# Sliding-window attention with a gated feed-forward: one P times V visit for two units, weights in half tiles

## The chip, the cores and the metric

One core of a Trainium2 chip. The metric is device microseconds of one execution, lower is better; times are medians of several runs. Engines are named as the profile names them: PE (TensorE) and PEld (its weight loads), DVE (VectorE), ACT (ScalarE), POOL (GpSimd), SP (SyncE, which issues nearly all DMAs here).

## The reference

All float32, T = 2048 tokens, D = 512, 32 heads of 16, window W = 256, F = 1792.

```python
xn = layernorm(x)                                   # no scale, no shift, eps 1e-5
q, k, v = split(xn @ wqkv)                          # 32 heads of 16
scores = q @ k.T / 4, kept where 0 <= i - j < 256   # else -1e9
s = concat_heads(softmax(scores) @ v) @ wo
f = (silu(xn @ w_gate) * (xn @ w_up)) @ w_down
return x + s * silu(f)
```

## The kernel before

**Precision.** A float32 matrix is split into two F32R tiles, high = copy to F32R (ACT) and low = value - high (POOL for weights and hidden tiles, DVE for what comes from PSUM). A product is three matmuls, the pairs (high, high), (high, low), (low, high) of `PAIRS`. P times V is done in plain float32, for which the trace shows two matmul records per call.

**Row halves.** PE is used as two halves of 64 rows, r = 0 and r = 1, that work side by side. Each dense item is summed in one bank, first by r = 0, then by r = 1 some `LAG` = 7 matmuls behind; a one-column DVE copy (`handover`, tile `ho`) separates the two. Weight tile j holds the upper input rows of unit j in partitions 0 to 63 and the lower ones of unit j - 1 in 64 to 127, so r = 0 reads tile n and r = 1 tile n + 1 during unit n.

**Dense work.** Tokens go in four chunks of 512. Per chunk there are 30 units in an order made by `dense_order`: `Proj` (q and k of a group of heads, tile a), `Values` (vp), `GateUp` (tiles g and u), `Down` (d, in four quarters of the hidden blocks and two halves of the output columns) and `Wo` (s). `Stationary` units (Proj, GateUp) hold weights in PE and move 512 tokens: item 0 uses the first 512 columns of the weight tile, item 1 the rest. `Moving` units (Values, Down, Wo) move 256 columns of weights, and both items use the whole tile. Each item takes one of four banks (`fb_free`).

**Weights.** `w_fetch` loads a raw tile (wr, 128 x 1024), `w_split` makes high (wh) and low (wl) of it in two or three cuts. Raw, high and low tiles all come from one pool of `NWB` = 10 tiles of 4 KB a partition; a pair is freed when both row halves are through with the unit (`unit_end`).

**Attention.** A unit u is four heads in one chunk, 32 units in all. For each: `max_pair` (scores b, row maxima on DVE, tile jk), `max_turn` (transposes the maxima, ms goes into q by a DMA of 8 KB), `prob_pair` (scores c with the maximum as an extra row, exponentials p on ACT, masks on POOL at L1325 and L1329), and `pv_visit` (P times V with v and a column of ones, L1390). All of these share four banks (`rb_free`). `pv_visit` uses PE as eight tiles of 64 x 32, issues all its matmuls in a row with nothing between them, and its two banks, one per row half, are added on the way out: copy on ACT (L1406), add on DVE (L1411), tile ev. ev goes to DRAM (od). The probabilities lie in one buffer of `PCAP` = 7168 columns: a unit's 6144, and 1024 more.

**Denominators.** `reciprocals` fetches the sums of two units from od, inverts them, stores them in rd. `o_prep` loads o from od and r from rd, and makes the operand of `Wo`.

**Order.** The program is a list in a fixed order on every engine, made ahead of time by a planner in the kernel itself. It keeps a virtual clock, costs per instruction, queues for DVE, ACT, POOL and DMAs ordered by due times (`do`, `dma`), and streams of attention visits with due times in units of dense work (`plan_attention`). An attention visit is put between dense matmuls when it is due and ready; dense work goes on where no visit is. Slots of 2 KB (`NSL` = 14, `take` and `give`) hold what lives for a short time.

Of the kernel before, what the change touches and what calls it, by code (L numbers as in the profile page):

```python
# [37 lines left out]
NHID = 8  # L38
PCAP = 7168
NSL = 14  # L40
NWB = 10
# [4 lines left out]
SPARE = 3  # L46
# [8 lines left out]
LEAD = 1.05  # L55
# [7 lines left out]
def tile_window_attention_swiglu_gate(  # L63
# [259 lines left out]
    def load_first():  # L323
# [66 lines left out]
        def split(raw, j, r, t):  # L390

            def high(a):
                if j not in wtile:
                    wtile[j] = [w_take(f"w{'hl'[s]}{j}", F32R) for s in range(2)]
                nc.scalar.activation(wtile[j][0][half(r), a : a + 512], raw[half(r), a : a + 512], AF.Copy)

            def low(a):
                hi, lo = (w[half(r), a : a + 512] for w in wtile[j])
                nc.gpsimd.tensor_tensor(lo, raw[half(r), a : a + 512], f32(hi), op=ALU.subtract)
                if r == 0 and a:  # L400
                    w_give(raw)

            def ready(t):
                if (j, r) == (1, 0):
                    low1.append(t)
                else:
                    wready[j] = t
# [12 lines left out]
        wr = [w_take(f"wr{j}", F32) for j in range(2)]  # L420
# [8 lines left out]
        split_next[0] = 2  # L429
# [48 lines left out]
    class Unit:  # L478
# [3 lines left out]
        def wts(self, r):  # L482
            return wtile[self.n + r]
# [10 lines left out]

    wfree = [f"w{i}" for i in range(NWB)]
    wheld = {}

    def w_take(name, dtype):
        tag = wfree.pop(0)
        t = pers.tile([P, 1024], dtype, name=name, tag=tag, bufs=1)  # L500
        wheld[id(t)] = (t, tag)
        return t

    def w_give(t):
        wfree.append(wheld.pop(id(t))[1])

    split_next = [0]

    def w_fetch(j):
# [8 lines left out]
        def go(r, u, last):  # L518
            if not box:
                box.append(w_take(f"wr{j}", F32))  # L520
# [7 lines left out]
        for n, (r, u) in enumerate(parts):  # L528
# [3 lines left out]
                slack=1.0, can=lambda: box or len(wfree) >= 3)  # L532

    def w_split(j, t, raw):
# [3 lines left out]
        if max(w) > both:  # L538
            r = 0 if w[0] > both else 1
            cuts += [(half(r), a, min(a + 512, max(w))) for a in range(both, max(w), 512)]  # L540
        if j not in weighted:
            cuts = [(half(1), 0, 256), (slice(0, P), 256, 768), (slice(0, P), 768, 1024)]
        left = [len(cuts), len(cuts)]

        def high(pr, a, b):
            if j not in wtile:
                wtile[j] = [w_take(f"w{'hl'[s]}{j}", F32R) for s in range(2)]
                split_next[0] += 1
            nc.scalar.activation(wtile[j][0][pr, a:b], raw[pr, a:b], AF.Copy)  # L549

        def low(pr, a, b):
            hi, lo = wtile[j]
            nc.gpsimd.tensor_tensor(lo[pr, a:b], raw[pr, a:b], f32(hi[pr, a:b]), op=ALU.subtract)  # L553
            left[1] -= 1
            if left[1] == 0:
                w_give(raw)

        def done(t):
            left[0] -= 1
            if left[0] == 0:  # L560
                wready[j] = t
# [7 lines left out]
        for n, (pr, a, b) in enumerate(cuts):  # L569
            do("S", t, 0.13 + 0.00078 * (b - a), lambda pr=pr, a=a, b=b: high(pr, a, b),  # L570
               lambda t, pr=pr, a=a, b=b, n=n: do(
                   "G", t, 0.17 + 0.0021 * (b - a), lambda: low(pr, a, b), done, before(MG, n)), before(MS, n),
               lambda: j in wtile or (split_next[0] == j and len(wfree) >= 2))


# [3 lines left out]
    def w_end(j):  # L579
        for t in wtile[j]:  # L580
            w_give(t)

    def unit_end(j, t):
        if (0, j) in half_ended and (j == 0 or (1, j - 1) in half_ended):
            timer(t, w_end, j)
# [53 lines left out]
    class Stationary(Unit):  # L639
# [7 lines left out]

        def gate(self, i, r, m):
            return xready.get((self.c, m // 3)) if self.n == 2 and i == 0 else 0.0

        def mms(self, i, r, pb):
            w = [t.rearrange("p (a k n) -> p a k n", a=2, k=KC) for t in self.wts(r)]
            xs = xn[self.c % 2]
            for k in range(KC):
                for a, b in PAIRS:
                    def go(first, last, k=k, a=a, b=b):
                        mm(pb, w[a][half(r), i, k, :], xs[b][half(r), k, :], first, last)
                    yield 512, go

    class Proj(Stationary):  # L660
# [7 lines left out]
        def done(self, i, pb, t, free):  # L668
# [3 lines left out]
            def high():  # L672
                tiles.extend(take(f"qk{'hl'[s]}{c}_{g}", dtype=F32R) for s in range(2))
                nc.scalar.activation(tiles[0], pb, AF.Copy)

            def low():
                nc.vector.tensor_tensor(tiles[1], pb, f32(tiles[0]), op=ALU.subtract)
# [7 lines left out]
            def after_high(t):  # L685
                do("V", t, 0.61, low, after_low, PRIO)
# [10 lines left out]
            do("S", t, 0.52, high, after_high, PRIO, can=room(2))  # L697

    class GateUp(Stationary):
# [8 lines left out]
        def done(self, i, pb, t, free):  # L708
# [7 lines left out]
            if i == 0:  # L716
                def tanh():
                    self.th = take(f"th{c}_{fb}")
                    self.y = take(f"y{c}_{fb}")
                    nc.scalar.activation(self.th, pb, AF.Tanh, scale=0.5)  # L720

                def one():
                    nc.vector.scalar_tensor_tensor(
                        self.y, self.th, 1.0, pb, op0=ALU.add, op1=ALU.mult
                    )
                    give(self.th)
# [5 lines left out]
                do("S", t, 0.5, tanh, lambda t: do("V", t, 0.61, one, after_one, PRIO), PRIO, can=room(2))  # L732
                return

            def product():
                self.h = take(f"h{c}_{fb}")
                nc.vector.scalar_tensor_tensor(
                    self.h, self.y, 0.5, pb, op0=ALU.mult, op1=ALU.mult
                )
                give(self.y)  # L740
# [17 lines left out]
            do("V", t, 0.61, product, after_product, PRIO, can=lambda: self.ty is not None and len(slots) >= 1 and hfree)  # L758
# [17 lines left out]
    class Moving(Unit):  # L776


        items = 2

        def mms(self, i, r, pb):
            w = [t[:, : self.width].rearrange("p (k n) -> p k n", n=256) for t in self.wts(r)]
# [941 lines left out]
```

## Time and profile before

| | us |
|---|---|
| median of 3 runs | 851.48 (850.3 to 852.09) |
| the profiled execution | 852.1 |
| its span, first to last instruction | 850.0 |
| PE busy | 842.0 |
| POOL busy | 629.5 |
| DVE busy | 502.7 |
| ACT busy | 487.3 |
| share of DMA queue q1 | 67.0% |

A row of a group reads: line, engine, operation, out<-in, shapes, count, then busy us and mean ns of one, then the idle time of the engine just before them and what ended it. A matmul counts as busy until its modelled end, and matmuls overlap, so PE can be busy all the time and still move more or fewer columns in a microsecond. A stretch of a window row gives its length, then busy time and count for each engine (in the order PE, PEld, DVE, ACT, POOL, or of the one engine asked for), then the granted clock, the DMA share and GB/s.

### The profile page before, as it was taken

The numbers are of one execution on the slowest core, as the hardware profiler recorded it, in microseconds if no ns is written. First come the engines' busy times: TensorE is split into PE (matmuls) and PEld (weight loads), VectorE is DVE, ScalarE is ACT, GpSimd is POOL, SyncE is SP. The second block draws the span as 40 slices with busy tenths as digits, with TensorE's granted clock in tenths as the row PEclk, the third lists the DMA queues.
The fourth block names the chain that finished last, engine by engine and source line by source line (L and its number), as shares of the span: only waits on it lengthen the run. The fifth ranks groups of instructions, "written<-read, shape, count | busy, mean of one in ns | idle before, by whom it ended". The sixth has DMA issues, their size and how long they took to land.

```text
span 850.0 us, 29939 instructions
## 1 busy us (share of the span) xinstructions
PE 842.0 (99%) x11946; PEld 786.6 (93%) x11946; DVE 502.7 (59%) x1676; ACT 487.3 (57%) x972; POOL 629.5 (74%) x909
## 2 busy tenths in 40 slices
PE   8999999999999999999999999999999999999998
PEld 8999999998998999989899999998999999899897
DVE  5355576655756766656656876466555677544235
ACT  6545656546566456545666556655556666565431
POOL 6566877867679697759787797767778878698871
PEclk9999999999999999999999999999999999999999
DMA  8478756585886986665858978566676868755233
GB/s 207 110 192 193 201 122 168 147 199 118 209 175 192 215 192 148 147 180 126 214 124 204 223 167 212 117 164 141 183 171 176 168 147 207 171 133 139 72 106 115
DMA packets 70226, 140.20 MB, mean 165 GB/s; under 512 B 14710, under 2 KB 23798, under 8 KB 70088
## 3 DMA queue, kind: packets, MB, share of 16 engines
q1 hardware_dynamic: 69624, 137.64, 67.0%
q8 instruction: 94, 1.54, 0.8%
q10 hardware_dynamic: 464, 0.66, 0.3%
q14 instruction: 44, 0.36, 0.2%
HBM read 107.94 MB, written 29.62 MB: 162 GB/s over the span
## 4 chain that ended last, share of the span: by engine, by line
PE 96%; DMA 2%; DVE 0%; ACT 0%; issue 0%; SPq 0%; DVEq 0%; ACTq 0%
PE d L593 18%; PE u L593 18%; PE g L593 18%; PE a L593 11%; PE pv L1390 8%; PE c L1353 6%; PE s L593 6%; PE vp L593 5%; PE b L1205 5%; DMA wr<-wgu 1%; DMA xt<-x 1%; DMA wr<-wdn 0%; PE xp L613 0%; DMA q<-ms 0%; PE xp L446 0%
## 5 line engine op out<-in xcount | busy, mean ns | idle before, releaser
L553 POOL TENSOR_TENSOR wl<-wr,wh 128x512 fp32r<-128x512 f32 (+2 forms) x261 | 306.2, 1187 | 74.4 <-ACT wh L549 50.8
L1213 DVE CUSTOM_DVE_ANT_0 jk<-b,maskb 128x384 bf16<-128x384 f32 (+2 forms) x512 | 271.4, 530 | 113.6 <-PE b L1205 66.5
L593 PE MATMUL d<-wh,hh 64*128 64x256 f32 x1792 | 269.4, 279 | 0.0
L1313 ACT ACTIVATE p<-c 128x512 f32<-128x512 f32 (+2 forms) x384 | 197.5, 572 | 99.1 <-PE c L1353 92.7
L593 PEld LDWEIGHTS d<-wh,hh 64*128 64x128 f32 x1792 | 230.7, 185 | 1.2 <-issue 0.4
L593 PE MATMUL d<-wl,hh 64*128 64x256 f32 x896 | 208.2, 279 | 0.0
L593 PE MATMUL u<-xl,wh 64*128 64x512 f32 x448 | 165.0, 393 | 0.0
L593 PE MATMUL u<-xh,wl 64*128 64x512 f32 x448 | 164.7, 393 | 0.0
L593 PE MATMUL g<-xl,wh 64*128 64x512 f32 x448 | 164.4, 393 | 0.0
L593 PE MATMUL g<-xh,wh 64*128 64x512 f32 x448 | 164.4, 394 | 0.0
L593 PE MATMUL g<-xh,wl 64*128 64x512 f32 x448 | 164.2, 393 | 0.0
L593 PE MATMUL u<-xh,wh 64*128 64x512 f32 x448 | 164.0, 394 | 0.0
L549 ACT ACTIVATE wh<-wr 128x512 fp32r<-128x512 f32 (+2 forms) x261 | 144.7, 588 | 14.5 <-POOL wl L553 5.6
L593 PEld LDWEIGHTS d<-wl,hh 64*128 64x128 f32 x896 | 146.8, 185 | 0.6 <-issue 0.2
L1325 POOL TENSOR_SCALAR_AFFINE_SELECT p<-p 128x256 f32<-128x256 f32 x256 | 101.2, 407 | 51.0 <-ACT p L1313 48.4
L748 POOL TENSOR_TENSOR hh<-h,hh 128x512 fp32r<-128x512 f32 x56 | 72.3, 1292 | 53.9 <-ACT hh L744 50.2
L1205 PE MATMUL b<-k,q 48*128 48x384 f32 (+2 forms) x512 | 107.6, 328 | 0.1
L1329 POOL TENSOR_SCALAR_AFFINE_SELECT p<-p 128x256 f32<-128x256 f32 x224 | 90.7, 407 | 18.0 <-ACT p L1313 17.3
L1353 PE MATMUL c<-q,k 49*128 49x128 f32 (+2 forms) x704 | 95.7, 299 | 1.0 <-DMA q<-ms 1.0
L593 PE MATMUL a<-xh,wh 64*128 64x512 f32 x256 | 96.5, 392 | 0.0
L593 PE MATMUL a<-xh,wl 64*128 64x512 f32 x256 | 96.0, 392 | 0.0
L593 PE MATMUL a<-xl,wh 64*128 64x512 f32 x256 | 95.9, 391 | 0.0
(117 smaller groups left out, 2109.6 us busy)
## 6 DMA issues: line engine op xcount, KB each, us to landing
wr<-wgu SPq DMA_DIRECT2D x112, 256.0 KB
k<-qkd SPq DMA_DIRECT2D x48, 192.0 KB
wr<-wqk SPq DMA_DIRECT2D x32, 256.0 KB
qkd<-qkh SPq DMA_DIRECT2D x32, 256.0 KB
qkd<-qkl SPq DMA_DIRECT2D x32, 256.0 KB
q<-qkd SPq DMA_DIRECT2D x64, 128.0 KB
wr<-wdn SPq DMA_DIRECT2D x32, 256.0 KB
od<-ev SPq DMA_DIRECT2D x32, 256.0 KB
```

The lines of the kernel that those rows point to most:

```text
L549: nc.scalar.activation(wtile[j][0][pr, a:b], raw[pr, a:b], AF.Copy)
L553: nc.gpsimd.tensor_tensor(lo[pr, a:b], raw[pr, a:b], f32(hi[pr, a:b]), op=ALU.subtract)
L593: return nc.tensor.matmul(pb, a, b, start=first, stop=last, skip_group_check=True)
L748: nc.gpsimd.tensor_tensor(hl[:, 1, :], self.h, f32(hl[:, 0, :]), op=ALU.subtract)
L1205: nc.tensor.matmul(pb[:, :n], qs[u % 3][r : r + 48, p, qb * P : (qb + 1) * P], ks[u % 3][r : r + 48, p, lo : lo + n], start=True, stop=True,)
L1213: nc.vector.tensor_tensor_reduce(junk[:, :n], pb[:, :n], maskb[:, 3 * P - n :], 1.0, -3.0e38, ALU.add, ALU.max, m[:, col : col + 1],)
L1313: nc.scalar.activation(t[:, h, :], pc[:, :n], AF.Exp, scale=DH ** -0.5)
L1325: nc.gpsimd.affine_select(s, s, [[0, 2], [1, P]], ALU.is_ge, 0.0, base=0, channel_multiplier=-1)
L1329: nc.gpsimd.affine_select(s, s, [[0, 2], [-1, P]], ALU.is_gt, 0.0, base=0, channel_multiplier=1)
L1353: nc.tensor.matmul(pc[:, at0 : at0 + w], ks[u % 3][r : r + 49, p, k0 : k0 + P], qs[u % 3][r : r + 49, p, qb * P : qb * P + w], start=(i == ...
L1390: nc.tensor.matmul(pbs[r][0][32 * j : 32 * j + 32, q0:q1], vt[half(r), (4 * c + kb) % VT, VW * (4 * g + j) : VW * (4 * g + j) + 32], t[hal ...
```

## The change

Four things, with the constants that go with them.

- **One visit for two units.** `pv_visit` is entered for odd u only and does units u - 1 and u one after the other. It needs four free banks of the ring instead of two. The probability buffer grows to 12288 columns, which is two units, and is empty after each visit.
- **Weights in half tiles.** High and low are tiles of 128 x 512, one pair for each half of the columns, ten such tiles (2 KB each) in place of the common pool; raw tiles have three places of their own. A half is ready by itself (`wready[j, h]`) and free by itself, after the last matmul that uses it (`used`): for a Stationary unit after the item, for a Moving unit in its second item. Moving units go over the first two blocks of the weights for both token blocks, then over the rest.
- **Gate-up in one tile.** tanh, the gate product and the product with up are written in place in one slot.
- **Denominators from the evicted tile.** After the add, a small DMA takes the four rows of sums of each unit straight from ev in SBUF into the tile of denominators; the fetch from od goes. o is loaded as soon as both units are stored, r when the reciprocals are.

Slots go from 14 to 10, hidden tiles from 8 to 7. `Values` of the chunks 1 to 3 are due a little later, which exchanges the first of them with the dense unit behind it in each of these chunks.

```diff
-NHID = 8
-PCAP = 7168
-NSL = 14
-NWB = 10
+NHID = 7
+PCAP = 12288
+NSL = 10
+NRAW = 3
+NWH = 10
...
-SPARE = 3
+SPARE = 2
...
-LEAD = 1.05
+LEAD = 1.06
...
+    def w_take(j, a):
+        if (j, a) in wtile:
+            return
+        tags = [wfree.pop(0) for _ in range(2)]
+        wtile[j, a] = [
+            pers.tile([P, 512], F32R, name=f"w{'hl'[s]}{j}_{a}", tag=tags[s], bufs=1) for s in range(2)
+        ] + tags
...
-                slack=1.0, can=lambda: box or len(wfree) >= 3)
+                slack=1.0, can=lambda: box or rfree)
...
-               lambda: j in wtile or (split_next[0] == j and len(wfree) >= 2))
+               before(MS, n),
+               lambda h=a // 512: (j, h) in wtile or (split_next[0] == (j, h) and len(wfree) >= 2))
...
+    def used(r, n, a, t):
+        half_ended.add((r, n, a))
+        j = n + r
+        if (0, j, a) in half_ended and (j == 0 or (1, j - 1, a) in half_ended):
+            timer(t, w_end, j, a)
...
     class Moving(Unit):
+        def gate(self, i, r, m):
+            return 0.0 if m < 12 else self.wat(r, 1)
...
+            n = self.width // 256
+            for ks in (range(2), range(2, n)):
+                for t in range(2):
+                    tok = slice((2 * i + t) * P, (2 * i + t + 1) * P)
+                    for k in ks:
+                        for a, b in PAIRS:
...
     class GateUp(Stationary):
-                    self.th = take(f"th{c}_{fb}")
-                    self.y = take(f"y{c}_{fb}")
-                    nc.scalar.activation(self.th, pb, AF.Tanh, scale=0.5)
+                    self.h = take(f"h{c}_{fb}")
+                    nc.scalar.activation(self.h, pb, AF.Tanh, scale=0.5)
...
-        dma(t, fetch, lambda t: do("V", t, 0.3, rec, lambda t: dma(t, back, landed_back, 0.5, 16)), 1.0, 16)
+        do("V", max(dens[c, k][1:]), 0.3, rec, lambda t: dma(t, back, landed_back, -5.0, 16), -1.0)
...
-        return None if t is None else latest([t, bank_time(rb_free, 2)])
+        return None if t is None else latest([t, bank_time(rb_free, 4)])
...
-    def pv_visit(u, es):
+    def pv_visit(u):
+        sums = [pv_unit(v) for v in (u, u + 1)]
+        advance(0.3 + sum(cost for _, cost in sums))
+        p_live.clear()
+        p_next[0] = 0
+        p_freed[0] = now[0]
+        for n in range(2):
+            halo_read.add(u + n)
+            pv_store(u + n, sums[n][0], 0.25 * n)
...
+        def sums():
+            k = c, g // 2
+            if k not in dens:
+                dens[k] = [sb(f"den{c}_{g // 2}", [P, 32], F32, "den", 2)]
+            move(dens[k][0][half(g % 2)], box[0][DH : P : 2 * DH].rearrange("j (a n) -> j a n", n=32))
...
+            dma(t, sums, after_sums, -5.0, 8)
             dma(t, store, after_store, -0.5, 256)
...
-            streams[1].append((u + 1.89, pv_ready, pv_visit, (u, tuple(range(ne)))))
+            if u % 2:
+                streams[1].append((u + 1.89, pv_ready, pv_visit, (u - 1,)))
...
-                timed.append((8 * c + 1.05 + 1.4 * hf if c else -9.0 + hf, Values(c, hf)))
+                timed.append((8 * c + 1.35 + 1.15 * hf if c else -9.0 + hf, Values(c, hf)))
```

More of the change, by code (lines that the diff above doesn't have):

```diff
@@ L419, in load_first @@
         rows(1, nc.scalar)
-        wr = [w_take(f"wr{j}", F32) for j in range(2)]
+        wr = [raw_take(f"wr{j}") for j in range(2)]
         u0, u1 = weighted[0], weighted[1]
@@ L756, in after_high @@
                 do("G", t, 1.24, low, lambda t: hready.__setitem__((c, fb), t), 1.0)
-            do("V", t, 0.61, product, after_product, PRIO, can=lambda: self.ty is not None and len(slots) >= 1 and hfree)
+            do("V", t, 0.61, product, after_product, PRIO, can=lambda: self.ty is not None and hfree)
     hid = {}
@@ L1107, in landed_back, with o_fetch, fetch, after @@
             o_prep(c, k)
-        dma(t, fetch, lambda t: do("V", t, 0.3, rec, lambda t: dma(t, back, landed_back, 0.5, 16)), 1.0, 16)
+        do("V", max(dens[c, k][1:]), 0.3, rec, lambda t: dma(t, back, landed_back, -5.0, 16), -1.0)
+    fetched = {}
+    def o_fetch(c, k):
+        at = latest(od_at.get(8 * c + 2 * k + n) for n in range(2))
+        if c not in o_open or at is None or (c, k) in fetched:
+            return
+        fetched[c, k] = []
+        def fetch():
+            fetched[c, k].append(take(f"o{c}_{k}"))
+            move(fetched[c, k][0], od[c, 8 * k : 8 * k + 8, :DH])
+        def after(t):
+            fetched[c, k].append(t)
+            o_prep(c, k)
+        dma(max(now[0], at), fetch, after, 0.5, 256, room(2 + (0 if c == NCH - 1 else SPARE)))
     def o_prep(c, k):
-        if c not in o_open or (c, k) not in rd_at or (c, k) in begun:
+        o_fetch(c, k)
+        if (c, k) not in rd_at or len(fetched.get((c, k), ())) < 2 or (c, k) in begun:
             return
@@ L1373, in pv_visit @@
         jobs = [[], []]
-        for e in es:
+        for e in range(3):
             for kb, qb, w, at0 in pieces(c, e):
@@ L1397, in pv_visit, with pv_store @@
             cost += both[0][0] * R * 0.00178
-        advance(cost)
-        p_live[:] = [l for l in p_live if l[2] != u]
-        p_freed[0] = now[0]
-        halo_read.add(u)
+        return pbs, cost
+    def pv_store(u, pbs, wait):
+        c, g = divmod(u, NG)
         box = []
@@ L1575, in next_mm @@
             work[0] += cols * MM / 512
+        if u.last_use(i) and all(o[2] != a for o in todo[m + 1 :]):
+            used(r, u.n, a, clock[r] + 0.2)
         run[r][1] += 1
```

223 lines of the change are left out of this document (110 added, 113 removed).

## The prediction

> **What bounds the kernel now.** I read the page first, then the waits of TensorE, then the chain of waits in order of time. The page's first rows:
>
> ```profile
> span 850.0 us, 29939 instructions
> PE 842.0 (99%) x11946; PEld 786.6 (93%) x11946; DVE 502.7 (59%) x1676; ACT 487.3 (57%) x972; POOL 629.5 (74%) x909
> PEclk9999999999999999999999999999999999999999
> PE 96%; DMA 2%; DVE 0%; ACT 0%; issue 0%; SPq 0%; DVEq 0%; ACTq 0%
> ```
>
> TensorE is busy for 842 of 850 us at the full granted clock, and 96% of the chain that ended last is TensorE's own work. So only two things can move the time: the time in which TensorE is counted busy without moving columns, and a new wait in front of it. The view of TensorE's waits shows how little waiting there is to win:
>
> ```profile
> PE warm L245 <- DVE warm L240: 1.1, 1, 1.1
> PE c L1353 <- DMA q<-ms: 1.0, 1, 1.0
> PE xp L446 <- DVE xt L347: 0.8, 1, 0.8
> PE xp L446 <- issue: 0.7, 1, 0.7
> PE s L593 <- DVE ho L590: 0.3, 1, 0.3
> ```
>
> These are all of its rows (total us, times, longest). Not one wait is for a split weight tile, for a bank or for a slot. Four of the five belong to the start or the very end. What is left is the busy time that does nothing, and for that I compare the pace in a plain stretch with the pace around a P times V visit. The chain gives the plain pace, two of the visits and the beginning of the last `Wo`:
>
> ```profile
> 535.29 2.38 PE pv L1390 x93
> 792.32 2.38 PE pv L1390 x93
> 816.44 14.86 PE d L593 x247
> 836.13 8.78 PE s L593 x143
> ```
>
> In the stretch from 816.44 a 256-column matmul takes 14.86 / 247 = 0.060 us, so two of them, one on each row half, start every 0.120 us.
>
> **One visit for two units: what a boundary costs.** The timeline of TensorE around the visit at 535.22, whose neighbours are `Down` matmuls of 256 columns:
>
> ```profile
> 534.90 0.35 PE L593 MATMUL d<-wl,hh 64*128 64x256 f32 x2
> 535.02 0.27 PE L593 MATMUL d<-wh,hh 64*128 64x256 f32 x1
> 535.22 2.45 PE L1390 MATMUL pv<-p,v 64*32 64x320 f32 x96
> 537.60 0.39 PE L593 MATMUL d<-wh,hh 64*128 64x256 f32 x2
> ...
> 537.83 0.38 PE L593 MATMUL d<-wh,hh 64*128 64x256 f32 x2
> ```
>
> From the last start before (535.02) to the second pair after (537.83) pass 2.81 us. Two steps of the plain pace are 0.24 of it. The rest is the visit's 96 matmuls and what the two changes of work cost. The matmuls run in twelve groups of eight: four of 320 columns, two each of 256, 192, 128 and 64. TensorE's count of pv matmuls in short stretches, cut where a group begins, gives the step of each size (16 in a stretch are eight that still run and eight that start):
>
> ```profile
> 535.50:535.77 0.27, 0.27 (x16) 1.00 0.00 0
> 536.31:536.53 0.22, 0.22 (x16) 1.00 0.00 0
> 536.74:536.90 0.16, 0.16 (x18) 1.00 0.00 0
> 537.07:537.17 0.10, 0.10 (x24) 1.00 1.80 205
> 537.28:537.36 0.08, 0.08 (x25) 1.00 0.69 154
> ```
>
> The steps go with the columns (0.27 / 320 = 0.84 ns a column), so the four 320s are 1.08, the pairs of 256, 192, 128 and 64 are 0.43, 0.33, 0.22 and 0.11, together 2.17 us. The fixed cost of the visit is 2.81 - 0.24 - 2.17 = 0.40 us. Beside 512-column neighbours it is the same:
>
> ```profile
> 414.97 0.39 PE L593 MATMUL g<-xh,wl 64*128 64x512 f32 x1
> 415.29 2.45 PE L1390 MATMUL pv<-p,v 64*32 64x320 f32 x96
> 417.67 0.50 PE L593 MATMUL g<-xh,wl 64*128 64x512 f32 x1
> ...
> 418.01 0.39 PE L593 MATMUL g<-xh,wh 64*128 64x512 f32 x1
> ```
>
> 3.04 us from 414.97 to 418.01, less two steps of 0.24 and 2.17, leaves 0.39. Part of it lies ahead of the visit's first matmul (0.20 from 535.02 to 535.22 in place of 0.12), part in the slow second pair behind it (0.23 from 537.60 in place of 0.12), the rest between the last pv matmul and 537.60.
>
> There are 32 visits, and after the change 16, so 16 boundaries go. What no row shows is the joint inside the doubled visit, where the 64-column groups of one unit are followed by the 320-column groups of the next into new banks. It costs between nothing and the whole 0.40. The nearest row is a group change inside a visit, which costs nothing beyond the columns for the large groups and, for the last 64-column ones, 0.08 in place of 0.054. I take 0.06 for the joint, nearer to that row: 16 x (0.40 - 0.06) = 5.4 us saved, between 0 and 6.4. [...]
>
> **Four banks at once.** The doubled visit waits for four free banks in the ring of scores and leaves all four full. From the groups, with the copies of weights and the masks for later use:
>
> ```profile
> L1406 ACT ACTIVATE ev<-pv 128x512 f32<-128x512 f32 x32 | 19.1, 597 | 59.6 <-PE pv L1390 53.8 <-issue 3.8 <-POOL wl L553 2.0
> L1411 DVE TENSOR_TENSOR ev<-ev,pv 128x512 f32<-128x512 f32 (+1 forms) x32 | 21.3, 667 | 31.9 <-ACT ev L1406 31.8
> L549 ACT ACTIVATE wh<-wr 128x512 fp32r<-128x512 f32 (+2 forms) x261 | 144.7, 588 | 14.5 <-POOL wl L553 5.6
> L553 POOL TENSOR_TENSOR wl<-wr,wh 128x512 fp32r<-128x512 f32 (+2 forms) x261 | 306.2, 1187 | 74.4 <-ACT wh L549 50.8
> L1325 POOL TENSOR_SCALAR_AFFINE_SELECT p<-p 128x256 f32<-128x256 f32 x256 | 101.2, 407 | 51.0 <-ACT p L1313 48.4
> ```
>
> Two copies in a row are 2 x 0.60 us, and the second add ends 0.67 us later, so scores can start again 1.2 us behind the visit and the ring is whole after 1.9; now it is 1.3. In this time TensorE has dense work, which uses four banks of its own, so I take nothing. If that cover were gone it would be 16 x 1.2 = 19 us. Attention as a whole gets later by perhaps that much over the run, but the last visit now ends at 794.7 and `Wo` of the last chunk, which needs it, starts at 836.13: 41 us of cover.
>
> **Denominators.** Sixteen fetches of 16 KB become 32 of 8 KB, whose nearest row is another 8 KB transfer, q<-ms:
>
> ```profile
> L102 SPq DMA_DIRECT2D den<-od x16: 597/654/664, 108.4 to 798.1; - x16
> 750.49 0.58 SPq L102 DMA_DIRECT2D q<-ms  x1
> ```
>
> On SP's queue that is 32 x 0.58 - 16 x 0.65 = 8.2 us more in 850, each put ahead of whatever is queued there, a q<-ms or a weight load. 0.58 us of delay per issue is hidden by the 41 us above and by weights that TensorE never waits for; if a q<-ms on the path met one each time, it would be 16 x 0.58 = 9 us, but in the waits that transfer held TensorE only once. I take nothing. One landing of od and one DMA round trip leave the chain to `Wo`, which was not late: no gain either. The gate-up pair keeps its tanh and its two DVE steps and only shares a tile: no time. The slots fall from 14 to 10 and the hidden tiles from 8 to 7; the latter just holds the seven blocks that stand before a chunk's first `Down`. A missing slot would hold a bank and then TensorE; its work is to be covered by the three other dense banks. I take nothing, and at worst a few us.
>
> **Half tiles.** Instruction counts stay: 261 copies and 261 subtractions. What shrinks is the lead. Ten tiles of 4 KB held up to four whole hi/lo pairs beside two raw tiles; now there are five half pairs and three raw tiles of their own. Where one `Moving` unit follows another, row half 0 and row half 1 keep four half pairs between them, and the second half of the tile after next can only be split once three quarters of the unit are done. A unit of 1024 is 96 x 0.060 = 5.8 us. What remains until row half 1 wants that half is a quarter of it (1.4 us), the lag of seven steps (7 x 0.23 = 1.6), and half an item (1.4): 4.4 us, more where attention runs between. The split needs 0.6 on ACT and 1.3 on POOL, 1.9 with no queue. So 2.5 us of queue on POOL, six masks of 0.41, may stand before it. POOL's worst stretch and three splits in it:
>
> ```profile
> 480.00:510.00 30.00, 30.00 (x442) 28.36 (x440) 24.05 (x77) 15.79 (x32) 27.10 (x49) 1.00 0.80 185
> 485.14 1.29 POOL L553 TENSOR_TENSOR wl<-wr,wh 128x512 fp32r<-128x512 f32 x1
> 499.99 1.29 POOL L553 TENSOR_TENSOR wl<-wr,wh 128x512 fp32r<-128x512 f32 x1
> 503.58 1.30 POOL L553 TENSOR_TENSOR wl<-wr,wh 128x512 fp32r<-128x512 f32 x1
> ```
>
> Here POOL is busy 27.1 of 30 us and makes no split for 13.6 us (486.4 to 500.0). The old lead carried TensorE over it with no wait; the new one will have to put splits into it and push masks back, which dense work hides. When a split is late, one row half stands still and the other goes on, so a us of lateness costs half. I bound this by -1.0 us (halves can be ready before a whole tile was, and raw loads no longer queue for pair tiles; the q<-ms wait of 1.0 is the only one in mid-run that could go) and +10 (below). I take +1.1, two late splits of about the size of the one mid-run wait in the table. The end of the run, 816 to 845, has no masks on POOL, so nothing there.
>
> **The sum.** -5.4 + 1.1 = -4.3 us. The profiled execution took 852.1 us (850.0 of span and 2.1 around it), 0.6 over the median of 851.48; it becomes 847.8, and the median 847.2.
>
> **Rivals.** (1) Late halves, ending slower. There are about 13 places with masks on POOL where `Moving` follows `Moving` (three `Down` pairs and a `Wo` pair a chunk, less those after 790). If at each of them row half 1 stands 1.2 us, that is 13 x 0.6 = 8 us: 851.5 - 5.4 + 8 = 854. It decides from 5.4 / 13 x 2 = 0.8 us a place. For it speaks POOL's 27.1 of 30; against it that the mean load of POOL is 74% and that the queue may reorder. (2) The joint costs as much as a boundary, so the change does not do what it says: 851.5. For it: no row shows a joint; against it: groups inside a visit follow one another at the pace of their columns. (3) Evictions bind. [...] In this kernel: four banks wait at once, dense work finds its own banks still full because ACT and DVE are at the pv banks, and TensorE stands 1.2 us a visit: 851.5 - 5.4 + 19 = 865. Against it, ACT is 57% and DVE 59% busy. (4) Everything helps: a free joint and 1.0 us of waits gone: 851.5 - 6.4 - 1.0 = 844.1.
>
> **How the numbers follow.** About 0.2% (1.7 us) can be told from no change. Chances: the forecast of 847.2, own range 844.5 to 849.8, 0.57; rival 4, 0.11; rival 2, 0.10; rival 1, 0.18; rival 3, 0.04. So faster 0.68, same 0.10, slower 0.22. The range runs from 843.8, just beyond rival 4, to 854, rival 1's own time, which leaves out half of rival 1, all of rival 3 and a little below.
>
> **What would show it.** Right: 16 pv visits of 192 or 128 matmuls in the chain, the c >= 1 ones 4.6 us long from first pv to first dense start; no gap at the middle; TensorE's waits still free of wl; the group times of POOL, ACT and DVE unchanged. Wrong: rows of TensorE waiting for wl or ev in that view, the chain passing through POOL splits, matmul means above 0.279 and 0.393 us, or doubled visits of 4.9 us.

## The result and the profile after

The changed kernel takes 861.49 us (median of four, 857.3 to 867.16), beside 851.48 for the kernel before. The ratio is 1.0116, with an interval of 1.007 to 1.0161: about 10 us slower, where 4.3 us faster was forecast. The profiled execution is the longest of the four, 867.16 us, with a mean granted clock of 0.991 where the others have 0.997 to 0.999, so its lost time, and the half clock shown below above all, is more than that of the median.

The first page of its profile, in the same rows as before:

```profile
span 865.4 us, 30089 instructions
PE 846.4 (98%) x11946; PEld 810.1 (94%) x11946; DVE 500.9 (58%) x1676; ACT 496.2 (57%) x972; POOL 630.7 (73%) x909
PEclk9999999999999899998999999999999999999999
PE 87%; DMA 7%; DVE 2%; POOL 2%; issue 1%; SPq 1%; ACT 0%; DVEq 0%; ACTq 0%; POOLq 0%
```

The instruction counts of TensorE, DVE, ACT and POOL are those of before, and so nearly is their busy time (POOL 630.7 for 629.5, DVE 500.9 for 502.7; ACT 496.2 for 487.3). What changed is that TensorE's share of the chain of waits fell from 96% to 87%, and that the granted clock shows two slices below 9. TensorE's waits, largest first, in the columns of the prediction's table:

```profile
PE s L608 <- issue: 3.4, 1, 3.4
PE d L608 <- POOL wl L568: 2.3, 1, 2.3
PE b L1244 <- DMA k<-qkd: 1.7, 2, 1.5
PE pv L1439 <- issue: 1.7, 2, 1.5
PE warm L246 <- DVE warm L241: 1.1, 1, 1.1
PE c L1392 <- DVE m L1252: 1.1, 1, 1.1
PE c L1392 <- DMA q<-ms: 1.0, 1, 1.0
...
PE d L608 <- issue: 0.6, 1, 0.6
```

One late half tile is there (POOL wl). The three "issue" rows are new: TensorE stood for nothing that the profile shows. No row waits for the copy or the add of ev. A long stall costs twice here, as stretches show (length, busy PE and PEld, and DVE, ACT and POOL, then the granted clock). First the changed kernel, then the kernel before:

```profile
284.00:288.00 4.00, 0.62 (x9) 0.51 (x8) 2.14 (x5) 1.36 (x3) 3.67 (x8) 0.77 0.76 239
288.00:293.00 5.00, 5.00 (x47) 5.00 (x48) 2.22 (x8) 0.00 (x0) 0.00 (x0) 0.50 0.31 78
407.00:412.00 5.00, 5.00 (x38) 5.00 (x37) 2.92 (x10) 1.09 (x2) 1.87 (x2) 0.50 1.05 210
```

```profile
284.00:288.00 4.00, 4.00 (x68) 4.00 (x67) 2.74 (x12) 2.12 (x4) 2.23 (x6) 1.00 1.07 252
288.00:293.00 5.00, 5.00 (x77) 5.00 (x75) 4.01 (x15) 3.21 (x6) 5.00 (x8) 1.00 1.08 190
```

After 3.4 us without work the next 5 us run at a granted clock of 0.50; it fell while TensorE still stood (0.54 from 286.00 to 287.80) and is 1.00 again from 293.00. The same follows the waits of 2.3 and 1.5 us, which end at 404.56 and 406.43 (0.50 from 406.40 to 412.40). The pause of 1.5 us that ends at 719.11 stands alone, and the clock behind it is 1.00 (719.10 to 724.00). How long a wait has to be for this is not shown.

The visits themselves did what was planned. The chain has nine of 4.62 to 4.73 us like the first row below, and the timeline gives the step:

```profile
473.70 4.65 PE pv L1439 x172
```

```profile
473.43 0.28 PE L608 MATMUL vp<-wh,xh 64*128 64x256 f32 x1
473.63 4.72 PE L1439 MATMUL pv<-p,v 64*32 64x320 f32 x192
478.28 0.38 PE L608 MATMUL d<-wh,hh 64*128 64x256 f32 x1
...
478.51 0.28 PE L608 MATMUL vp<-wh,xl 64*128 64x256 f32 x1
```

From 473.43 to 478.51 pass 5.08 us. Less two plain steps (0.24) and twice the columns (4.34) that is 0.50, so the joint costs 0.10 beside a boundary's 0.40. If all 16 joints are like this one, that saves 16 x 0.30 = 4.8 us, near the forecast. Other costs took this back and 10 us more.

### The profile page after: what moved, and what is told of

It is laid out like the page before. It is cut to its first block, busy times and chain, and to the rows that moved or that the text cites. A ratio compares the mean times of both kernels' runs of the same rounds, so it can differ in the third digit from the quotient of the medians.

```text
span 865.4 us, 30089 instructions
## 1 busy us (share of the span) xinstructions
PE 846.4 (98%) x11946; PEld 810.1 (94%) x11946; DVE 500.9 (58%) x1676; ACT 496.2 (57%) x972; POOL 630.7 (73%) x909
## 4 chain that ended last, share of the span: by engine, by line
PE 87%; DMA 7%; DVE 2%; POOL 2%; issue 1%; SPq 1%; ACT 0%; DVEq 0%; ACTq 0%; POOLq 0%
PE g L608 17%; PE d L608 16%; PE u L608 16%; PE a L608 10%; PE pv L1439 8%; PE c L1392 6%; PE vp L608 5%; PE b L1244 5%; PE s L608 4%; DMA k<-qkd 2%; DMA wr<-wgu 2%; DMA q<-ms 1%; DVE jk L1252 1%; DMA q<-qkd 1%; DMA qkd<-qkl 1%
## 5 line engine op out<-in xcount | busy, mean ns | idle before, releaser
L608 PE MATMUL d<-wh,hh 64*128 64x256 f32 x1792 | 262.8, 279 | 0.6 <-issue 0.6
L608 PEld LDWEIGHTS d<-wh,hh 64*128 64x128 f32 x1792 | 226.0, 186 | 0.4
L563 ACT ACTIVATE wh<-wr 128x512 fp32r<-128x512 f32 (+2 forms) x261 | 152.3, 589 | 94.5 <-PE d L608 32.0
L608 PE MATMUL d<-wl,hh 64*128 64x256 f32 x896 | 203.8, 278 | 2.3 <-POOL wl L568 2.3
L608 PE MATMUL u<-xl,wh 64*128 64x512 f32 x448 | 162.2, 392 | 0.0
L608 PE MATMUL u<-xh,wl 64*128 64x512 f32 x448 | 161.8, 392 | 0.0
L608 PE MATMUL g<-xh,wh 64*128 64x512 f32 x448 | 160.9, 393 | 0.0
L608 PE MATMUL u<-xh,wh 64*128 64x512 f32 x448 | 160.5, 391 | 0.0
L608 PE MATMUL g<-xl,wh 64*128 64x512 f32 x448 | 160.5, 392 | 0.0
L1244 PE MATMUL b<-k,q 48*128 48x384 f32 (+2 forms) x512 | 111.8, 334 | 2.4 <-DMA k<-qkd 1.7
```

The source lines that it names most:

```text
L563: nc.scalar.activation(wtile[j, h][0][pr, a - 512 * h : b - 512 * h], raw[pr, a:b], AF.Copy)
L608: return nc.tensor.matmul(pb, a, b, start=first, stop=last, skip_group_check=True)
L1244: nc.tensor.matmul(pb[:, :n], qs[u % 3][r : r + 48, p, qb * P : (qb + 1) * P], ks[u % 3][r : r + 48, p, lo : lo + n], start=True, stop=True,)
```

## The experiments

Four theories. **S**: SP, whose list has a fixed order, waits for the three places of raw tiles and holds other loads back. **H**: less weight memory gives less lead, the time between a split and its use. **V**: the visits to two units cost time beside what they save. **T**: any new planned order costs a few us against this one.

### The doubled visit and the raw tiles in the changed kernel

The change makes SP wait for POOL's subtractions far more (SP's waits; the kernel before, then the changed one):

```profile
SPq L102 <- POOL wl L553: 38.4, 24, 9.4
```

```profile
SPq L103 <- POOL wl L568: 222.6, 91, 8.5
```

e1 gives a raw tile back later in the plan, so that the plan queues fewer loads behind it.

```diff
-            if left[2] == 0:
-                raw_give(raw)
+            if left[2] == 0:                  # when the subtraction has ended
+                timer(t + 0.5, raw_give, raw)
```

> The changed kernel, but a raw weight tile counts as free to the planner 0.5 us after the planned end of its last subtraction instead of at its start; nothing else differs. In the profile of the changed kernel SP's queue waited 222.6 us (91 times) for a POOL subtraction, against 38.4 us (24 times) before. Theory S (the next weight load stands at the head of SP's queue until POOL has let go of the raw tile, and the loads of q, k, ms and weights behind it come late): SP's wait for POOL wl falls under 60 us and the time falls from 861.5 to 846 to 851, with no TensorE stall over 2 us in mid-run. Theory H (five half pairs are too few, whoever loads): SP's wait falls all the same, the time stays at 858 to 863. Theory V (the doubled visit stalls TensorE itself, by its instruction supply or its four banks): 858 to 863 and the stalls stay next to the visits.

Measured: 871.29 us, ratio 1.0224 (1.0189 to 1.0259), worse than the change. SP's wait fell from 222.6 to 149.2 us only, not under 60, so S is not decided by this run.

e2 takes the doubled visit back (single visits, 2 banks, `PCAP` 7168) and keeps all else of the change.

```diff
-            if u % 2:
-                streams[1].append((u + 1.89, pv_ready, pv_visit, (u - 1,)))
+            streams[1].append((u + 1.89, pv_ready, pv_visit, (u,)))
```

> The changed kernel with one visit for each unit again, two banks, probability buffer of 7168 columns; half tiles, raw ring, gate-up and denominators as in the change. Theory S: the SP waits stay near 220 us and the time is 861.5 plus the 16 boundaries, 860 to 868. Theory H: the same. Theory V: the stalls go, 848 to 854.

Measured: 857.74 us, 1.0079 (1.0051 to 1.0108). By the medians the doubling costs 3.8 us instead of saving 4.8. The interval overlaps that of the changed kernel (1.0070 to 1.0161), so that it costs something is not clear of noise here; that it does not save 4.8 is.

e4 is e2 with the freed memory given to weights.

```diff
-NRAW = 3
-NWH = 10
+NRAW = 5
+NWH = 16
```

> One visit for each unit as in the run beside it, and the 20 KB that this frees given to weights: five raw tiles instead of three and sixteen half tiles instead of ten. Theory S: with five raw tiles the next load is asked for later than POOL needs, SP's wait for POOL wl falls under 80 us, the time to 849 to 853. Theory H: the lead is as long as before the change, 849 to 853 as well, and ACT's wait for TensorE before a copy falls from 61 us under 20. Theory V: like the run beside it.

Measured: 865.33 us, 1.0162 (1.0146 to 1.0177). More memory made it slower, so H does not hold in this form.

e7 is e4 with a load only when three raw places are free; e8 is e2 with raw tiles given back 3 us after the subtraction.

```diff
-                slack=1.0, can=lambda: box or rfree)
+                slack=1.0, can=lambda: box or len(rfree) >= 3 - (j < 5))
```

> Single visits, half tiles, five raw tiles and sixteen halves, as in the run that had 865.3, but a load is only asked for when three raw tiles are free, so that it takes one that has been free for some time, as the common pool did before. Theory S: SP's wait for POOL wl falls from 150.7 to under 50 us and the time to 849 to 854. Theory H or a third cause: SP's wait falls, the time stays at 860 to 866.

```diff
-                raw_give(raw)
+                timer(t + 3.0, raw_give, raw)
```

> Single visits, half tiles and three raw tiles, as in the run that had 857.7, but a raw tile counts as free 3 us after the planned end of its last subtraction. Theory S: SP's wait for POOL wl falls from 205 to under 60 us and the time to 850 to 854. Theory H: SP's wait falls, ACT's wait for TensorE before a copy stays at 60 us or more, the time at 856 to 860.

Measured: e7 858.64 us (1.0091, 1.0074 to 1.0108), e8 857.45 us (1.0070, 1.0049 to 1.0092). In e8 the wait of SP fell to less than a third of e2's, and the time is the same:

```profile
SPq L103 <- POOL wl L568: 205.3, 89, 6.8
```

```profile
SPq L104 <- POOL wl L569: 63.0, 36, 5.9
```

The first row is e2, the second e8. S is a real wait, but cutting it to a third gains nothing beside single visits with three raw places. With five places (e4 to e7) the wait fell from 150.7 to 22.8 us and the time by 6.7 us; but e7 also leaves about three of the five places in use, as e2 has, so this does not tell the wait from the number of loads ahead.

### The doubled visit on the weights of before

e5 gives the kernel before a raw ring of three (and `NWB` 8, `NHID` 7). e9 has `NWB` 8, one-tile gate-up and the smaller `NSL` and `NHID`, with single visits. e6 is e9 with doubled visits and the changed due times of `Values`.

```diff
-NWB = 10
+NWB = 8
+NRAW = 3
...
-                box.append(w_take(f"wr{j}", F32))
+                box.append(raw_take(f"wr{j}"))
```

> The kernel before with one part of the change alone: raw tiles have three places of their own, given back as the subtraction starts; eight whole tiles of high and low instead of the common ten, seven hidden tiles instead of eight. Theory S: SP's wait for POOL wl rises from 38 to 150 us or more and the time to 855 to 862. Theory H: four whole pairs remain, so no change, 850 to 853. Theory V: no change, 850 to 853.

```diff
-NHID = 8
-NSL = 14
-NWB = 10
+NHID = 7
+NSL = 10
+NWB = 8
```

> The same memory as the run beside it (eight weight tiles, ten slots, seven hidden tiles, gate-up in one tile) with a visit for each unit. Theory S (what costs is a weight load that waits at the head of SP's queue for a raw tile just being read): the common pool still hands out the tile that has been free longest, SP's wait for POOL wl stays under 90 us, time 851 to 856. Theory H (a shorter lead costs by itself): 856 to 864, with TensorE standing at splits.

```diff
-        return None if t is None else latest([t, bank_time(rb_free, 2)])
+        return None if t is None else latest([t, bank_time(rb_free, 4)])
...
+        sums = [pv_unit(v) for v in (u, u + 1)]
```

> The kernel before with the doubled visit as its one change of order; to make room for the larger probability buffer the gate-up pair shares a tile, the common weight pool has eight tiles instead of ten, slots are ten and hidden tiles seven. No half tiles, no raw ring, denominators as before. It is to be read against the run beside it, which has the same memory and single visits. Theory V (a doubled visit uses up TensorE's instructions faster than they are fetched): 16 boundaries save 5 to 7 us, stalls of 1 to 4 us that end 1.3 to 1.8 us after a 16 KB packet of the instruction queue take 4 to 12 back, so equal to the run beside it or up to 6 us slower. Prediction's own sum: 5.4 us faster than the run beside it.

Measured: e5 861.47 us (1.0122, 1.0105 to 1.0139), e9 867.37 us (1.0185, 1.0162 to 1.0208), e6 878.65 us (1.0328, 1.0303 to 1.0354). Apart from a unit that looks up its weights later, e9 differs from f2 below (852.85) only in eight tiles for ten in the weight pool, and is 14.5 us slower. So less weight memory costs here, as H has it and by more than H's 856 to 864, though TensorE's waits for wl are only 1.0 us in all: how it costs is open. e5 has three raw places beside its eight tiles, eleven tiles for ten; SP's wait for POOL rose to 169.2 us and the time lies where S put it (855 to 862), not where H did. Doubling costs 11.3 us more than e9, clear of noise, and e6 names a place (its waits, and one of its visits):

```profile
PE pv L1392 <- issue: 5.8, 5, 2.8
```

```profile
390.72 2.42 PE L1392 MATMUL pv<-p,v 64*32 64x320 f32 x80
395.90 0.35 PE L1392 MATMUL pv<-p,v 64*32 64x64 f32 x16 [2.76 <-issue]
```

TensorE stops for 2.76 us in the middle of a visit, and the profile shows nothing that it waits for. The page's list of queues has a row that did not matter so far, the same in both kernels:

```profile
q8 instruction: 94, 1.54, 0.8%
```

94 packets of 16 KB. By its name, and by the pauses that follow here, I take it for TensorE's own instruction stream; the 23,892 matmuls and weight loads of the program, divided by 94, would then be 254 to a packet, an estimate. In the trace of the changed kernel packets of this queue end at 286.28 and 717.55, and TensorE goes on 1.52 and 1.56 us later, at 287.80 and 719.11. The table counts, in the one profiled execution of each, the pauses of over 0.7 us from one matmul's start to the next that the waits put to "issue" and that end 1.1 to 1.9 us behind such a packet:

| kernels | doubled | single | difference of the medians |
|---|---|---|---|
| after, e2 | 3 pauses, 6.4 us | none | +3.8 us |
| e1, e8 | 8 pauses, 16.2 us | none | +13.8 us |
| e6, e9 | 6 pauses, 11.1 us | 1 pause, 0.9 us | +11.3 us |

(e1 and e8 differ also in when the raw tile is given back.) The kernel before has none. Past the first 10 us, every "issue" pause of this length in all the profiles ends so soon behind a packet, which ties the pauses to this queue. The other versions with single visits have none or one of up to 1.1 us; h1 and h2 below, with four pairs joined, have one of 1.9 and two of 4.0 together. Three times visits of 384 instructions in 4.65 us came with more pauses than single ones, and the price grows roughly with their sum. That they are the price is not shown by it.

f5 is e6 with at least 2.8 us of dense work between the two units, so that no burst of 384 is left; f6 is f5 with 2 banks asked for ahead of each unit.

```diff
+        if u % 2 and pos[0] < len(stream) and work[0] < pv_work[0] + 2.8:
+            return None
...
-        return None if t is None else latest([t, bank_time(rb_free, 4)])
+        return None if t is None else latest([t, bank_time(rb_free, 2 if u % 2 else 4)])    # f6: always 2
```

> The doubled visit of e6 on the memory of before, but with at least 2.8 us of dense work between its two units: the probabilities of both units are still awaited before the first, and only the 384 instructions in one burst are gone. Theory V by instruction supply (a burst of 384 short instructions outruns the fetches of TensorE's instructions): no wait in a visit that follows a 16 KB fetch, and 866 to 870 us, as e9 with single visits has 867.4. Theory V by late probabilities and four banks: 875 to 880, as e6 with 878.7.

> f5 (two units' probabilities awaited, then two visits with dense work between: 883.2) with 2 banks asked for ahead of each visit, not 4 ahead of the first. If the four banks cost it: 867 to 871, near e9 with single visits (867.4). If it is the lateness of the first unit's visit, held until the second unit's probabilities are there: 878 to 885.

Measured: f5 883.18 us (1.0369, 1.0342 to 1.0395), f6 869.11 us (1.0200, 1.0166 to 1.0234). f5 went against my expectation: its visits have no such pause any more and it is still slower than e6. f6, with the four banks gone too, comes back to within 1.7 us of e9, and its row is down to this:

```profile
PE pv L1397 <- issue: 0.6, 1, 0.6
```

So awaiting two units' probabilities costs little with this memory; 14 us between f5 and f6 belong to the four banks where the visits are apart. How e6's own 11.3 us divide between pauses and banks these runs do not say: the pauses alone are as long as the difference, but f5 shows that without them the banks can cost as much.

### The rest of the change, one part at a time

All of these are the kernel before with one edit: f1 the denominators, f2 gate-up in one tile with 10 slots, 7 hidden tiles and a spare of 2, f3 the lead and the due times of `Values`.

```diff
+            dma(t, sums, after_sums, -5.0, 8)          # f1
             dma(t, store, after_store, -0.5, 256)
...
-NSL = 14
+NSL = 10                                              # f2
...
-LEAD = 1.05
+LEAD = 1.06                                           # f3
```

> The kernel before, with one part of the change alone: denominators taken straight from the evicted tile, the quotients' loads ahead of the reciprocal. The changed kernel with single visits still loses 6 us to the kernel before, and this run says whether that lies in the denominators. Prediction's reading (0 for this part): 850 to 853 us. If the added small transfers on SP's queue hold weight loads back: 854 to 857 and more SP waits. Theory T (any re-planning of the written-out order costs a few us, whatever is changed): 853 to 857, with waits of TensorE on changing releasers and no group of this part among them.

> The kernel before, with gate-up in one tile, 10 slots for 14, 7 hidden tiles for 8, a spare of 2 for 3, nothing else. Prediction's reading (0 for this part): 850 to 853 us. If fewer slots and hidden tiles hold work back: 854 to 858, with TensorE's u or d groups waiting for hh or for a bank that VectorE frees late. Theory T: 853 to 857 with no group of this part among the waits.

> The kernel before, with the lead of 1.06 for 1.05 and the due times of the Values stages of the changed kernel, and no other edit: the same instructions in another planned order. It is the control for theory T. If the due times as such are harmless: 850 to 853 us. If any re-planning of this order costs something on the chip: 853 to 858, and then a few us of the changed kernel's loss belong to no part of it.

Measured, against 851.94: f1 857.52 us (1.0074, 1.0057 to 1.0091), f2 852.85 us (1.0022, 1.0002 to 1.0042), f3 852.37 us (1.0024, 1.0004 to 1.0044). T falls as a rule for any new order: these two cost 0.9 and 0.4 us by the medians, at most a few tenths of a per cent. The denominators alone cost 5.6 us, clear of noise. e2 (857.74) is only 0.2 above f1, so if the parts added up, half tiles, slots and order would be nearly free beside them. No run has the half tiles without the denominators and with single visits, and h2 below speaks against adding up.

The chain of waits and SP's timeline show a part of f1's loss. The chain of f1 has two pieces that the kernel before has not:

```profile
607.80 9.90 DMA q<-ms
631.84 6.95 DMA q<-ms
```

An 8 KB transfer, the row maxima that scores c need, is on the path for 9.9 us. TensorE has dense work for most of that time, so the path is much longer than the stall; in f1's waits this transfer has 1.9 us:

```profile
PE c L1363 <- DMA q<-ms: 1.9, 3, 1.0
```

All waits of TensorE together grew by 1.8 us (3.9 to 5.7) while the span grew by 5.0, so 3 us of the loss are slower work that no wait names. SP's issues ahead of it in f1, then in the kernel before:

```profile
604.46 0.62 SPq L102 DMA_DIRECT2D o<-od  x1
605.13 1.32 SPq L102 DMA_DIRECT2D r<-rd  x1
606.50 0.57 SPq L102 DMA_DIRECT2D o<-od  x1
607.11 0.59 SPq L102 DMA_DIRECT2D r<-rd  x1
607.80 0.57 SPq L102 DMA_DIRECT2D q<-ms  x1
```

```profile
603.80 1.08 SPq L102 DMA_DIRECT2D r<-rd  x1
604.93 0.57 SPq L102 DMA_DIRECT2D o<-od  x1
605.60 0.57 SPq L102 DMA_DIRECT2D q<-ms  x1
606.21 0.58 SPq L102 DMA_DIRECT2D o<-od  x1
606.84 1.38 SPq L102 DMA_DIRECT2D r<-rd  x2
```

With the quotient's loads no longer in a chain, a second broadcast of 256 KB (r) has moved ahead of q<-ms, which is issued 2.2 us later. But ScalarE makes ms 1.9 us later too (606.50 for 604.60), so f1 was late here already, and the queue's order adds only the rest. In the kernel before the packets ended 8.7 us behind the issue, 0.95 us ahead of the first c; in f1 they ended 9.3 us behind it, and TensorE stood 0.54 us.

g1 puts that chain back and keeps the sums from the evicted tile. g2 leaves f1 as it is and lets ScalarE, which makes ms, issue q<-ms on its own queue; g4 does the same to the kernel before.

```diff
-        dma(max(now[0], rd_at[c, k]), fetch_r, then_r, -1.0, 256, room(1))
+        dma(max(now[0], rd_at[c, k]), fetch_o, then_o, 0.5, 256, room(2 + (0 if last else SPARE)))
```

> f1 (denominators straight from the evicted tile, 857.5) with one thing taken back: the quotient's operands are loaded one after the other once the reciprocals are back, as in the kernel before, not the first tile early and the broadcast at once. In f1's chain of waits an 8 KB transfer of the score rows' maxima (q<-ms) stands for 9.90 and 6.95 us, and at 607 us a 256 KB broadcast r<-rd stands ahead of it on SP's queue that in the kernel before comes after it. If that order is what costs f1 its 5.6 us: 851 to 853. If the small transfers and the urgent places of the denominators cost it: 856 to 859.

```diff
-            move(qs[u % 3][48 : 113 : 64], box[0])
+            move(qs[u % 3][48 : 113 : 64], box[0], nc.scalar)
...
-            dma(t, put, lambda t: ms_at.__setitem__(u, t), -3.0, 8)
+            dma(t, put, lambda t: ms_at.__setitem__(u, t), -3.0, 8, e="S")
```

> f1 with the transfer q<-ms issued by ScalarE, which makes its tile, on a queue of its own, not by SP behind the 256 KB transfers. If f1 loses through scores that wait for this transfer: 852 to 854, no wait c<-DMA q<-ms left, and no transfer q<-ms of more than 3 us. If these waits are only where the lateness of something else shows: 856 to 858, with the wait moved to other rows.

> The kernel before with the same single edit (q<-ms on ScalarE's queue), the control for g2 and a try at a faster kernel. It has one such wait, of 1.0 us: 850.5 to 852.5 if ScalarE bears the 32 issues beside its other work (487 us busy of 850); 853 to 857 if they make its other work late.

Measured: g1 855.31 us (1.0046, 1.0027 to 1.0065), g2 873.78 us (1.0200, 1.0146 to 1.0254), g4 865.00 us (1.0142, 1.0117 to 1.0167). g1 takes back 2.0 of the 5.6 us, but its interval overlaps f1's: the order of the quotient's loads is perhaps a part, and 3.6 us remain with the sums' own 32 issues and the urgent places, which no run separates. g2 (two of its six runs at about 863 us, four at 873 to 876) and g4 are slower. ScalarE can now stand at the issue until an earlier transfer has landed, and its other work with it. In g4 this happens three times, for 7.0, 4.1 and 6.0 us; the second of them in its timeline:

```profile
518.90 0.27 ACT L1254 ACTIVATE ms<-mt 16x128 fp32r<-16x128 f32 x1
519.08 0.37 ACT L631 ACTIVATE xh<-xp 128x256 fp32r<-128x256 f32 x1
522.94 0.52 ACTq L102 DMA_DIRECT2D q<-ms  x1
523.51 0.38 ACT L631 ACTIVATE xh<-xp 128x256 fp32r<-128x256 f32 x1 [4.06 <-DMA wr<-wqk]
```

### Both parts taken out of the changed kernel

h1 is the changed kernel with 2 banks asked for ahead of each unit, the second unit behind the first; h2 is h1 with the denominators of before.

```diff
-        return None if t is None else latest([t, bank_time(rb_free, 4)])
+        return None if t is None else latest([t, bank_time(rb_free, 2)])
```

> The changed kernel with its visit to two units left as it is in time (both units' probabilities awaited, the second unit right behind the first where it can), but 2 banks asked for ahead of each unit, not 4 ahead of both: f6's edit on the changed kernel, with no dense work forced in between. If the four banks cost the changed kernel what they cost on the memory of before (14 us there, less here): 853 to 858, below the single visits of e2 (857.7) by what is left of the joints' gain. If the doubling costs through its burst of instructions: 860 to 863, as the changed kernel's 861.5, with waits of TensorE in visits again.

> h1 with the denominators as in the kernel before (fetched back from DRAM, the quotient's loads in a chain): the best combination the runs so far point to. If the 5.6 us of f1 are paid in the changed kernel too: 848 to 853 where h1 has 853 to 858, that is 4 to 6 us below h1. If they are only what any new order costs beside the kernel before: within 1.5 us of h1.

Measured: h1 867.53 us (1.0213, 1.0175 to 1.0251), h2 860.55 us (1.0101, 1.0088 to 1.0114). h1 lies above both of its forecasts. Without the wait for four banks most pairs came apart, as the chain of h2 shows:

```profile
374.94 2.38 PE pv L1429 x93
378.21 2.38 PE pv L1429 x93
```

So little of the joints was left, and the units still waited for each other; h1 does not tell the price of the four banks in the changed kernel. It is also 9.8 us above e2, whose single visits await one unit and likewise ask for 2 banks, though it has only one pause of 1.9 us: in the changed kernel, awaiting two units may be what costs. The price of the denominators shows again: taking them out gave 7.0 us (5.6 in f1). But h2, with neither them nor the four banks, is still 8.8 us above the kernel before, where its forecast was 848 to 853. These 8.8 us are not explained. No version beat the kernel before.

## Why the prediction was wrong

- **Denominators at nothing.** This step failed, by 5.6 us (f1) to 7.0 us (h1 to h2), both clear of noise. The prediction priced 0.58 us of SP's time per issue and dismissed it because q<-ms held TensorE only once before. It did not look at how little was to spare at that transfer (8.7 us in flight at 605.60, and 0.95 us from its end to the first c), nor at what else moves ahead of it when the quotient's loads leave their chain. The waits for q<-ms grew only from 1.0 to 1.9 us of the 5.0 by which f1's span grew; how the rest is lost is open.
- **Saved by the joints, 5.4.** The step itself was right: 4.8 by the prediction's own reckoning, with a joint of 0.10 for 0.06.
- **The visit as a whole.** Here the -5.4 failed as a price. It counted columns, boundaries and banks, and took for granted that TensorE's next instruction is always there. In place of a saving the doubling cost 3.8 us by the medians (after against e2, intervals overlap) and 11.3 us clear of noise (e6 against e9). "No gap at the middle" was the line that would show trouble, and the row of 1.7 us at pv answers it. How the cost divides between the pauses, the four banks and the wait for two units' probabilities stays open.
- **Four banks at nothing.** Doubtful: they cost 14 us in f5 against f6, in another setting, although the prediction had 41 us of cover for later attention; open in the changed kernel.
- **Half tiles at +1.1, slots and gate-up at 0.** The late half is there once, a wait of 2.3 us in the changed kernel's profile. Slots and gate-up alone cost 0.9 by the medians (1.0002 to 1.0042). The half tiles have no run of their own; 0.2 for all of these holds only if the parts add up, and 8.8 us of h2 say that they may not.
- **Rivals.** Rival 1 ended on the right side, but with one late half in the table where it had about 13. At that one neither row half went on: no matmul begins between 401.89 and 404.56, so a us of lateness cost a us there, not the half that the prediction took. Rival 2 fell, since the joint cost 0.10 where a boundary costs 0.40. Rival 3 had TensorE standing 1.2 us a visit for the evictions; no such wait is in the table, though four banks may cost by making a visit late, as in f5.

## What to carry to other kernels

A row without waits says what waited, not how much was to spare; before something is put ahead of a small transfer on a shared queue, measure for each of its uses how long it was in flight and how soon it was needed. When an edit joins short bursts of small matmuls to long ones, count their instructions per microsecond too, and look for pauses of TensorE that end soon behind a packet of the instruction queue (1.1 to 1.9 us here). Run each part of a bundle alone: here one that was priced at nothing cost 5.6 us. And do not take the parts for a sum: what is left without the costly ones has to be run too.

## What the runs showed of the hardware

- The page lists a queue q8, called instruction, beside those of the data, with 94 packets of 16 KB. That they are TensorE's instructions, about 254 matmuls and weight loads each, is my reading and an estimate (23,892 / 94). In the changed kernel TensorE paused three times with no cause that the profile shows (waits of 0.6, 3.4 and 1.5 us put to "issue") and went on 1.35, 1.52 and 1.56 us after such a packet had ended. From the start of the packet before to the start of this one 478, 425 and 382 matmuls and weight loads had begun. The number alone does not decide it, since the kernel before reached 390 and 398 (behind the packets that start at 259.69 and 760.37) without such a pause.
- The 8 KB transfer q<-ms took 1.44 to 8.71 us from its issue to the end of its last packet in the kernel before (2.7 on average), 1.43 to 9.10 in the changed one (3.2). On a queue of its own it was not always short: in g4's chain it stands for 7.25, 6.28 and 7.13 us. There ScalarE's other work waited ahead of the issue too (7.0, 4.1 and 6.0 us).
- In the changed kernel a pause of 3.4 us, and two shorter ones of 2.3 and 1.5 us close together, were followed by 5 and 6 us at a granted clock of 0.50; one of 1.5 us alone was not.
